# Sliding-window attention and an MLP on one core: another order of the first six blocks, and another queue for weights and casts

## The chip, the cores and the metric

The kernel runs on one core of one Trainium2 chip. The metric is the time of one execution in device microseconds, given as the median of several runs. TensorE (PE in the profile) does the matrix products and the transposes, VectorE (DVE), ScalarE (ACT) and GpSimd (POOL) do the element-wise work, and SyncE (SP) only issues transfers. GpSimd issues transfers too, on a queue of its own; only its transfers can convert fp32 to fp16 on the way.

## The reference

The inputs are q, k and v of shape (8, 8, 576, 64) in fp32: 8 sequences, 8 heads, 576 positions, 64 columns per head. The attention is causal with a window of 128 positions and a linear bias for each head. Its result, all heads side by side, gives x of shape (8, 576, 512), which goes through a normalised two-layer MLP with a residual.

```python
scores = scale * np.matmul(q, k.transpose(0, 1, 3, 2))
bias = slopes[:, None, None] * (-np.abs(rel).astype(np.float32))[None, :, :]
mask = (rel >= 0) & (rel < window)                  # window = 128
attn = softmax(np.where(mask, scores + bias[None], -1e9))
x = np.matmul(attn, v)                              # then heads side by side: (B, S, 512)
xn = (x - mu) / np.sqrt(var + 1e-06) * g_ln         # over the 512 columns
out = x + np.maximum(xn @ w_ch1, 0.0) @ w_ch2       # 512 -> 2048 -> 512
```

## The kernel before

**Blocks.** The 8 x 576 positions are cut into 36 blocks of 128 rows. Nine blocks (PERIOD) are a pair of sequences: with r the block's number within the pair, r from 0 to 3 are rows of the first sequence, r = 4 is half of either sequence, r from 5 to 8 are rows of the second one. Because of the window a block looks only at itself and at the block before it; with r = 0 there is none before it, and the block has half the work in scores, exponentials and P·V.

**Attention of a block** (function `attention`). q and k must stand with the head's columns on the partitions (tile qkt). This is reached in one of three ways. In a *span* (`SPANS`, lines 608 to 656) two neighbouring blocks are loaded together by SP into fp32 tiles qs and ks, so that one run in memory is 512 bytes (line 459); they are cast to fp16 (line 621, written `cT`), two fp16 values are taken as one fp32 word and transposed by PE (line 639, `T`), and copied out of PSUM (lines 648 and 650). A block outside the spans and below `LOAD_CAST` is loaded by SP (line 364), cast (line 560), and transposed by PE (line 687); from `LOAD_CAST` on, q and k are loaded as fp16 by GpSimd's queue (line 473), and from `QK_BY_DMA` on the transposition is a DMA transpose on SP's queue (line 702). v is loaded by SP and cast (lines 591 and 593) below `V_CAST`, and comes as fp16 by GpSimd's queue into tile vx from there on. The scores are written to the PSUM tiles sc0 and sc1 (line 725). For the first `BY_BIAS` = 5 blocks the bias is added by matrix products with a distance table (line 741); later blocks multiply the exponentials (line 773) by a mask (line 780). P·V (line 797) carries a column of ones, so that the sum of a row comes with it; its reciprocal (line 814) and the division (line 818) give xb, 16-bit. The mean is subtracted and the gain g multiplied (line 858, tile xs), and xs is transposed to xt, by PE for blocks below `X_BY_DMA` (lines 872 to 882) and by a DMA transpose on SP's queue from there on (line 887).

**The MLP** (function `mlp`) works on chunks of 2 to 4 blocks (`CHUNKS`). Phase A multiplies the chunk's xt by 16 slices of the first matrix (line 919, tasks `A`), with ReLU on ScalarE or VectorE (lines 929 and 931); phase B multiplies by the second matrix (line 947, tasks `B`), and line 955 scales by the standard deviation's inverse and adds the residual. The division by the standard deviation thus comes after both products. Each matrix comes in four quarters on GpSimd's queue, w0 to w3 for the first and w4 to w7 for the second. `W_AFTER` gives behind which load or cast each quarter is issued: position 3 i is q of block i, 3 i + 1 is k, 3 i + 2 is v.

**The order** of all instructions is made when the program is built. Every step is a task with an engine, a cost, what it depends on and a priority; class `Plan` runs through the tasks with these costs in an event loop, and the order in which it starts them is the order in each engine's queue. On the chip the engines wait for semaphores, but never change this order. `PICK` names the engines that may do a task, `PRI` shifts priorities, `HOLD` keeps a task back until a time of the plan, `SLACK` is a reserve after what PE waits for, and `rates` and `LANDING` stand for the speed of the transfer queues. Before `WARM`, PE's planned pauses are filled with products of a zero tile (line 986, L986 in the profile). Rings of tiles (class `Ring`) give block i the tile i modulo the ring's length; a write waits for the readers of the tile's last owner.

## Time and profile before

| | |
|---|---|
| time, median of 6 runs | 320.26 us (319.88 to 321.63) |
| the profiled execution: its time | 320.56 us |
| the profiled execution: its span | 318.8 us |
| PE busy | 308.6 us, 97% of the span |
| products of the MLP (L919, L947) | 135.7 + 135.7 us |
| P·V (L797), scores (L725, two groups) | 28.4, 19.7 + 18.4 us |
| products of the zero tile (L986) | 7.4 us, 76 of them |
| granted PE clock | 0.999 |

The page shows the span of one execution, which is a little shorter than its time. An engine's busy time is the union of its instructions; for PE it contains the products of the zero tile, which compute nothing. A wait is told with the engine and line that waited, and what ended the wait. "to landing" of a transfer runs from its issue to the moment its data are there. POOLq and SPq are the instructions with which GpSimd and SyncE issue transfers.

### The profile page before, as it was taken

The page shows a single profiled execution, that of the slowest core. Times are in us where ns is not written, and L with a number is a line of the kernel's source. Part 1 is how long each engine was busy: PE and PEld are TensorE (multiplying, and loading weights), DVE is VectorE, ACT ScalarE, POOL GpSimd, SP SyncE. Part 2 cuts the span into 40 slices and gives each one's busy share as a digit, 9 for nine tenths or more (in the row PEclk, how much of TensorE's full clock was granted, in tenths as well). Part 3 has the DMA queues.
Part 4 walks back from the last instruction along what each step waited for, and adds up shares of the span by engine and source line. Part 5 has one row for each costly group of instructions (what it writes and reads, how often), then busy time and mean ns, then how long its engine had stood idle before and what let it go on. Part 6 is the DMA issues. An engine that isn't in the chain of part 4 may idle for free.

```text
span 318.8 us, 6461 instructions
## 1 busy us (share of the span) xinstructions
PE 308.6 (97%) x2526; PEld 174.9 (55%) x2526; DVE 184.8 (58%) x511; ACT 164.6 (52%) x269; POOL 98.9 (31%) x131
## 2 busy tenths in 40 slices
PE   8969989999999999999999999999999999999995
PEld 6746866556655554554555545554555455445543
DVE  3669558874599648664866486548664866111012
ACT  2759875445656742474257525752575257305600
POOL 5735476673564256353433231001000000000000
PEclk9999999999999999999999999999999999999999
DMA  8999999999999999999999998627710221011011
GB/s 197 233 189 230 210 210 174 156 184 174 157 141 168 150 174 161 182 185 147 164 213 99 100 165 166 50 49 135 131 19 16 85 82 19 17 68 67 0 66 68
DMA packets 153906, 41.47 MB, mean 130 GB/s; under 512 B 138385, under 2 KB 148881, under 8 KB 153874
## 3 DMA queue, kind: packets, MB, share of 16 engines
q0 software_dynamic: 91232, 15.34, 68.8%
q1 hardware_dynamic: 62640, 25.70, 42.2%
q8 instruction: 20, 0.33, 0.5%
q14 instruction: 12, 0.10, 0.1%
q10 hardware_dynamic: 2, 0.00, 0.0%
HBM read 36.70 MB, written 9.44 MB: 145 GB/s over the span
## 4 chain that ended last, share of the span: by engine, by line
PE 86%; DMA 7%; SPq 5%; POOL 0%; issue 0%; DVE 0%; POOLq 0%
PE fb L947 39%; PE fb L919 36%; PE sc L725 5%; PE fb L797 5%; DMA w1sb<-in_moe_w_ch_dram 5%; SPq L364 3%; DMA qs<-in_q_dram 3%; SPq L459 2%; PE fb L872 1%; PE fb L639 0%; POOL vx L473 0%; POOL qs L621 0%; DVE ot L955 0%; POOLq L621 0%
## 5 line engine op out<-in xcount | busy, mean ns | idle before, releaser
L919 PE MATMUL fb<-xt,w1sb 128*128 128x512 f16 (+2 forms) x640 | 135.7, 359 | 1.0 <-DMA w1sb<-in_moe_w_ch_dram 1.0
L947 PE MATMUL fb<-w2sb,ht 128*128 128x512 f16 (+2 forms) x592 | 135.7, 373 | 0.0
L931 ACT ACTIVATE ht<-fb 128x512 f16<-128x512 f32 (+2 forms) x145 | 80.9, 560 | 62.9 <-PE fb L919 61.7
L773 ACT ACTIVATE probs<-sc 128x1024 f16<-128x1024 f32 (+1 forms) x72 | 67.6, 973 | 54.8 <-PE sc L725 54.7
L919 PEld LDWEIGHTS <-w1sb 128*128 128x128 f16 x640 | 68.3, 114 | 47.7 <-DMA w1sb<-in_moe_w_ch_dram 1.2
L947 PEld LDWEIGHTS <-ht 128*128 128x128 f16 x592 | 54.1, 98 | 56.9
L955 DVE SCALAR_TENSOR_TENSOR ot<-fb,rstd,xb 128x512 f32<-128x512 f32 (+2 forms) x37 | 27.2, 736 | 53.9 <-PE fb L947 53.3
L473 POOL DMA_DIRECT2D vx<-in_v_dram x34 | 28.8, 847 | 71.1 <-PE fb L797 64.0
L780 DVE TENSOR_TENSOR probs<-probs,mreg 128x1024 f16<-128x1024 f16 (+1 forms) x48 | 31.4, 656 | 28.7 <-ACT probs L773 28.4
L797 PEld LDWEIGHTS <-probs 128*128 128x128 f16 x544 | 25.4, 98 | 14.1 <-ACT probs L773 0.4
L818 DVE SCALAR_TENSOR_TENSOR xb<-fb,rec 128x256 f16<-128x256 f32 x72 | 30.5, 423 | 2.0
L473 POOL DMA_DIRECT2D qk<-in_q_dram x30 | 25.4, 846 | 18.5 <-DMA qkt<-qk 6.5
L473 POOL DMA_DIRECT2D qk<-in_k_dram x30 | 25.4, 846 | 12.5 <-DMA vx<-in_v_dram 5.7
L797 PE MATMUL fb<-vx,probs 128*128 128x65 f16 x544 | 28.4, 193 | 0.1
L858 DVE SCALAR_TENSOR_TENSOR xs<-xb,mean,g_t 128x512 f16<-128x512 f16 x36 | 27.4, 761 | 0.7
L839 DVE BATCH_NORM_STATS2 st<-xb 128x6 f32<-128x512 f16 x36 | 24.5, 683 | 0.0
L814 DVE RECIPROCAL rec<-fb 128x4 f32<-128x4 f32 x72 | 13.0, 180 | 19.4 <-PE fb L797 18.8
L725 PEld LDWEIGHTS <-qkt 64*128 64x128 f16 x544 | 15.3, 94 | 12.3 <-issue 10.5
L725 PE MATMUL sc<-qkt 64*128 64x128 f16 x288 | 19.7, 216 | 0.0
L725 PE MATMUL sc<-qkt,qkt 64*128 64x128 f16 x256 | 18.4, 219 | 0.0
L929 DVE TENSOR_SCALAR ht<-fb 128x384 f16<-128x384 f32 (+2 forms) x15 | 8.5, 565 | 5.1 <-PE fb L919 4.3
L621 POOL CAST qs<-qs 128x512 f16<-128x512 f32 (+1 forms) x7 | 6.3, 899 | 9.8 <-DMA qs<-in_q_dram 9.8
(62 smaller groups left out, 120.7 us busy)
## 6 DMA issues: line engine op xcount, KB each, us to landing
out_dram<-ot SPq DMA_DIRECT2D x35, 256.0 KB, 3.5
vx<-in_v_dram POOLq DMA_DIRECT2D x28, 128.0 KB, 9.7
qk<-in_q_dram POOLq DMA_DIRECT2D x24, 128.0 KB, 11.0
qk<-in_k_dram POOLq DMA_DIRECT2D x24, 128.0 KB, 11.0
w1sb<-in_moe_w_ch_dram POOLq DMA_DIRECT2D x4, 512.0 KB, 10.7
w2sb<-in_moe_w_ch_dram POOLq DMA_DIRECT2D x4, 512.0 KB, 12.5
ks<-in_k_dram SPq DMA_DIRECT2D x6, 256.0 KB, 4.6
qs<-in_q_dram SPq DMA_DIRECT2D x6, 256.0 KB, 4.9
```

Source lines behind the costliest of these rows:

```text
L473: nc.gpsimd.dma_start(out=dst(p0, n), in_=src[b, :, s0 : s0 + n, :].rearrange("h p d -> p h d"))
L725: nc.tensor.matmul(scs[half][:, g, c0 : c0 + P], kt[rows, 1, hp, :], qkt[i][rows, 0, hp, :], start=not bias, stop=True, skip_group_check=True,
L773: nc.scalar.activation(out=o, in_=n_, func=AF.Exp, scale=inv_sqrt_d)
L780: en.tensor_tensor(out=pv, in0=pv, in1=mask[:, 2 * half : 2 * half + 2, :, lo:], op=ALU.mult)
L797: nc.tensor.matmul(pp[:, hh * (D + 1) : hh * (D + 1) + D + 1], probs[i][:, bank, slot, side * P : side * P + P], vx[i - 1 + side][:, h, 0 ...
L818: nc.vector.scalar_tensor_tensor(out=xb[i][:, 256 * half : 256 * half + 256].rearrange("p (h d) -> p h d", d=D), in0=pp[:, :, 0:D], scalar ...
L839: nc.vector.bn_stats(out=st[i][:, :], in_=xb[i][:, :])
L858: nc.vector.scalar_tensor_tensor(out=xs[i][:, :], in0=xb[i][:, :], scalar=mean[i][:, 0:1], in1=g_t[:, :], op0=ALU.subtract, op1=ALU.mult,)
L919: nc.tensor.matmul(fb[b][:, 0:n_], w1f[f // CB][:, kb, f % CB, :], xt[c][:, kb, 0:n_], start=(kb == 0), stop=(kb == NKB - 1),)
L931: nc.scalar.activation(out=ht[c][:, f, 0:n_], in_=src, func=AF.Relu)
L947: nc.tensor.matmul(pm[:, 0 : c1 - c0], ht[c][:, f, j * P : j * P + P], w2sb[f // CB][:, f % CB, c0:c1], start=(f == 0), stop=(f == NFB - 1),)
L955: nc.vector.scalar_tensor_tensor(out=ot[i][:, c0:c1], in0=fb[plan.held[key][1]][:, 0 : c1 - c0], scalar=rstd[c][:, j : j + 1], in1=xb[i][: ...
```

## The change

The blocks are worked on in another order. `BLOCK[i]` is the block at place i: first blocks 0 and 1, 9 and 10, 18 and 19 (the first two of the first three pairs of sequences, `HEADS` = 3), then all others in their order. Whatever is indexed by place stays so (rings, chunks, spans); memory addresses, r and the block before go through `BLOCK` and `PLACE`. The tiles vx and qkt of places 1, 3 and 5, whose next block comes much later, are pinned, outside their rings.

The places 0 to 5 are three spans (`SPANS` from [0, 2, 5, 7] to [0, 2, 4]). From place 6 on q and k come as fp16 by GpSimd's queue (`LOAD_CAST` from 9 to 6), and v from place 1 on (`V_CAST` from 5 to 1). The weights' quarters are issued behind v2, v3 (four), v4 (two) and k6 (`W_AFTER`). q and k of places 6 to 11 are transposed by PE (`QK_BY_DMA` from 9 to 12), and xs by DMA from place 6 on (`X_BY_DMA` from 12 to 6). The first chunks are 3, 3 and 2 blocks instead of 3, 2 and 3. The tables `PICK` (engines per task), `PRI` and `HOLD` are others, and some costs of the plan: the shares of the queues, landing times of the first four places, the first transposition, the first quarter of weights, `SLACK` after 30 us from 0.2 to 1.0 and `WARM` from 22 to 24.

```diff
 class Ring:
+    def __init__(self, tiles, pins=None):
+        self.tiles, self.first, self.readers, self.pins = tiles, {}, {}, pins or {}
+    def turn(self, k):
+        return k - sum(1 for p in self.pins if p < k)
     def __getitem__(self, k):
-        return self.tiles[k % len(self.tiles)]
+        return self.pins[k] if k in self.pins else self.tiles[self.turn(k) % len(self.tiles)]
...
+    SHARES = {
+        (True, 512): (0.83, 0.28), (True, 256): (0.75, 0.2), (True, 2048): (0.7, 0.4),
+        (False, 512): (0.38, 0.62), (False, 256): (0.5, 0.5), (False, 2048): (0.5, 0.5),
+    }
...
-    CHUNKS = [3, 2, 3, 4, 4, 4, 4, 4, 4, 4]
+    CHUNKS = [3, 3, 2, 4, 4, 4, 4, 4, 4, 4]
...
-    WARM = 22.0
+    WARM = 24.0
...
-    MIX_AFTER = 4
+    MIX_AFTER = 3
     SPLIT = 4
-    LOAD_CAST = 9
-    V_CAST = 5
+    LOAD_CAST = 6
+    V_CAST = 1
...
-    SPANS = [0, 2, 5, 7]
-    SLACK = (0, 0.2, 0)
+    SPANS = [0, 2, 4]
+    SLACK = (0, 1.0, 0)
...
+    HEADS = 3
     BY_BIAS = 5
     MASK_AT = 5
-    QK_BY_DMA = 9
-    X_BY_DMA = 12
+    QK_BY_DMA = 12
+    X_BY_DMA = 6
...
+    BLOCK = [b for n in range(HEADS) for b in (PERIOD * n, PERIOD * n + 1)]
+    BLOCK += [b for b in range(NBLK) if b not in BLOCK]
+    PLACE = {b: i for i, b in enumerate(BLOCK)}
+    FAR = [i for i, b in enumerate(BLOCK) if b + 1 < NBLK and (b + 1) % PERIOD and PLACE[b + 1] > i + 1]
...
-    v32 = ring("v32", min(5, V_CAST), [P, H, D], FP32)
-    qk16 = ring("qk16", 6, [P, 2, d_model], FP16)
-    vx = ring("vx", 7 if V_CAST > 4 else 9, [P, H, VD], FP16)
-    qkt = ring("qkt", 6, [P, 2, HP, P], FP16)
+    v32 = ring("v32", min(4, V_CAST), [P, H, D], FP32)
+    qk16 = ring("qk16", 5, [P, 2, d_model], FP16)
+    vx = ring("vx", 7 if V_CAST > 4 else 9, [P, H, VD], FP16, FAR)
+    qkt = ring("qkt", 6, [P, 2, HP, P], FP16, FAR)
...
-        b0, r = 2 * (i // PERIOD), i % PERIOD
+        b0, r = 2 * (BLOCK[i] // PERIOD), BLOCK[i] % PERIOD
...
-    W_AFTER = [6, 12, 17, 18, 21, 22, 22, 28]
+    W_AFTER = [8, 9, 10, 10, 10, 12, 12, 19]
...
-            t_w[n] = plan.transfer(f"w{n}", "POOL", 0.8, 3.2 if n < 4 else 2.7, 0.0, emit, [casts[at % 3]] + last, av(i, -60.0))
+            t_w[n] = plan.transfer(f"w{n}", "POOL", 0.8, (3.2 if n else 4.2) if n < 4 else 2.7, 0.0, emit, [casts[at % 3]] + last, av(i, -60.0))
...
-        r = i % PERIOD
+        r = BLOCK[i] % PERIOD
+        before = PLACE[BLOCK[i] - 1] if r else None
...
-                                kt = qkt[i - 1 + side]
+                                kt = qkt[i if side else before]
...
-                            vx[i - 1 + side][:, h, 0 : D + 1],
+                            vx[i if side else before][:, h, 0 : D + 1],
...
-                    nc.sync.dma_start(out=out_flat[i * P : i * P + P, c0:c1], in_=ot[i][:, c0:c1])
+                    nc.sync.dma_start(out=out_flat[BLOCK[i] * P : BLOCK[i] * P + P, c0:c1], in_=ot[i][:, c0:c1])
```

## The prediction

> **What bounds the kernel now.** I read the page first: which engine has no slack, and when.
>
> ```profile
> span 318.8 us, 6461 instructions
> PE 308.6 (97%) x2526; PEld 174.9 (55%) x2526; DVE 184.8 (58%) x511; ACT 164.6 (52%) x269; POOL 98.9 (31%) x131
> ...
> PE   8969989999999999999999999999999999999995
> ...
> DMA  8999999999999999999999998627710221011011
> ...
> PE 86%; DMA 7%; SPq 5%; POOL 0%; issue 0%; DVE 0%; POOLq 0%
> ```
>
> PE is full from the sixth slice (8 us each) to the last. A change to the order can only win what PE loses in the first 42 us, where the chain leaves PE. The chain in order of time names the places, and the waits of PE (us in total, times, longest) and its timeline (start, duration) size them:
>
> ```profile
> 17.16 8.21 DMA qs<-in_q_dram
> ...
> 27.06 14.63 DMA w1sb<-in_moe_w_ch_dram
> 41.74 2.14 PE fb L919 x12
> ```
>
> ```profile
> PE fb L687 <- POOL qk L560: 2.7, 1, 2.7
> PE fb L639 <- POOL qs L621: 1.1, 2, 0.7
> PE fb L986 <- DVE warm_t L376: 1.1, 1, 1.1
> PE fb L919 <- DMA w1sb<-in_moe_w_ch_dram: 1.0, 1, 1.0
> PE fb L872 <- DVE xs L858: 0.7, 1, 0.7
> ```
>
> ```profile
> 4.30 0.76 PE L741 MATMUL sc<-dist_t,sid 128*128 128x128 f16 x8
> ...
> 22.92 0.40 PE L687 MATMUL fb<-iden,qk 128*128 128x128 f16 x4 [2.74 <-POOL qk L560]
> ...
> 25.25 0.84 PE L919 MATMUL fb<-xt,w1sb 128*128 128x384 f16 x4
> ...
> 41.74 2.14 PE L919 MATMUL fb<-xt,w1sb 128*128 128x384 f16 x12 [0.98 <-DMA w1sb<-in_moe_w_ch_dram]
> ```
>
> Read: first useful matmul at 4.30, first MLP matmul at 25.25, dense after 41.74. The filler (L986) hides losses that the page counts as busy. Between 4.3 and 41.74 I add the gaps and the stretches of filler: 4.6 us of filler and small waits up to 23.3, 2.9 around the late k cast of block 4 (22.92), 0.74 at 26.83, 0.98 at 41.74: **9.3 us lost**. The last matmul ends 3.4 us before the end. So the span is 4.3 + 301.8 (PE's real work) + 9.3 + 3.4 = 318.8.
>
> **The change, part by part.** The sum is made against the profiled execution (span 318.8, time 320.56, which lies 0.30 above the median of 320.26).
>
> *PE's work.* Bias matmuls (L741) are made for places 0 to 4 in both kernels. Before, these are one block without a predecessor and four with one: 0.60 (4.30 to the next instruction at 4.90) + 4 x 1.06 (four matmuls of 256 columns go from 9.54 to 10.07) = 4.8. After, three are without and two with: 3.9. So -0.9. Transposes of q and k on PE: four spans at 0.92 (12.42 to 12.88 is half of one) and one plain block at 0.46 before; three spans and six plain blocks (places 6 to 11, L687) after: 4.1 to 5.5, so +1.4. Transposes of xs (L872): twelve blocks to six, 0.28 each (0.23 to 0.33 in the timeline), -1.7. Scores and P·V keep their number, since four blocks in 36 have no predecessor in either order. Sum **-1.2**: 300.6. The six extra copies out of PSUM (L697, 1.02 on ScalarE) and six copies fewer of xt (0.4 to 0.6) lie beside PE, with ScalarE 22.3 us busy of the 40 between 60 and 100; without that cover they cost some 2 us.
>
> *DMA.* Landing times of before (issue plus time to landing): halves of a span (256 KB) come 0.9 to 1.1 us apart while SP's queue is alone (3.9, 4.75, 5.85, 7.0; 10.2, 11.0, 12.0, 12.9), v by SP 1.04 and 1.26, a casting load of 128 KB by POOL 0.85 (50.9, 51.7, 52.55), a quarter of W2 alone 2.3 and 2.6 (45.1, 47.4, 50.0). The four quarters of W1 land at 21.9, 28.2, 35.0 and 41.7; in the 19.8 us from the first to the last, three of them, two v and eight halves land, so a W1 quarter beside SP costs (19.8 - 8 x 0.95 - 2 x 0.85)/3 = 3.5.
>
> Of POOL's queue, the dependencies give the order v1, v2, w0, v3, w1 to w4, v4, w5, w6, v5, q6, k6, w7 (places, not blocks). Ahead of w3's landing stand twelve halves (11.4), v0 (1.1), v1 to v3 (2.6) and four quarters (14): 29.1 after a start at 2.9, so **w3 lands at 32**, 9.7 us earlier than now, w4 at 34.5, w5 38, w6 40, v5 41, w7 45 (now 55.0). The price stands in front: the halves of the second span now share the engines with v1, v2 and w0. The last of them lands at 12.9 now. After: 8 halves and v0 are 8.7, v1 and v2 1.7, so 13.3 if no weight gets ahead, and 17.7 if w0 and v3 do (+3.5 +0.85). POOL issues in order at 0.53 to 0.92 each: whatever cast of qs or ks stands behind such an issue is late by it, and the thirteen weights and v issued here pass POOL's casts of the second span. POOL also waits for old transfers: in the trace a q issue at 55.74 waits 1.65 for w7, the transfer eight issues earlier; in the new order the one eight before v4 is v1, landed long ago, so this costs nothing before 41.
>
> The Trainium skill (DMA: Bandwidth & Descriptors, Specifications) puts line rate at 512 B and more and a read-modify-write below, which speaks against casting loads whose rows are 128 B in SBUF. The 0.85 against 1.04 to 1.26 for uncast rows of 256 B shows no such cost here; were each of the five v twice a plain load (2.3), w7 would be 7 us later by that estimate.
>
> *When the MLP begins.* From the landing of the second span's last half to the third block's xt, the chain of before is 12.9 to 21.3 (xs of its third block ends at 20.46, transposition and copy 0.8): 8.4, with a full block and full ScalarE. After, the third block has no predecessor: cast 0.8, transposes 0.45, copy 0.6, scores 0.28, exp 0.6, P·V 0.13, reciprocal and division 0.7, mean 0.2, xs 0.75, transpose and copy 0.75, with waits about 6. So the MLP starts between 13.3 + 6 = 19.3 and 17.7 + 1.2 (a share of w1) + 8.4 = 27.3. Neither end is nearer to a row, so I take the middle, **23.4** (now 25.25).
>
> *Loss.* By then PE can have done G 1.1, two spans 1.8, bias 3.9, scores of four blocks 1.7, P·V of four 1.5, three xs transposes 0.8: 10.8. Lost: 23.4 - 4.3 - 10.8 = 8.3. The other limit is w3: before 32 PE has in addition three quarters of chunk 0 (16 matmuls go from 28.21 to 30.81, 2.6 each) and 2.0 of attention, 20.6 in all: 32 - 4.3 - 20.6 = 7.1, less than 8.3, so it doesn't bind. After that each W2 quarter (2.5) feeds 2.6 us of chunk 0, and v5 at 41 gives chunk 1 by about 45, when w7 lands. For a mismatch of a fixed order with such narrow margins I add 0.7 (before: 0.74 + 0.98 after its start); ends 0 and 2.5. X = **9.0** instead of 9.3.
>
> The Trainium skill (SBUF — State Buffer, SBUF: two separate sides) says that VectorE's two-port operations keep GpSimd from writing descriptors, so its DMAs wait. Rows: issues between 25 and 42, with VectorE busy 11.7 of 16.5 us, take 0.53 to 0.92, the later ones 0.85 to 0.93. By the rule, thirteen issues each behind half a cast of 0.46 would add an estimated 3 us.
>
> Sum: 4.3 + 300.6 + 9.0 + 3.4 = **317.3**, 1.5 less than 318.8; as a median **318.8**.
>
> **Rivals.**
> *The queue of weights makes the first chunk late (slower).* Place: SP's q and k of the second span against w0 and v3. For it: w0 to w3 land 6.3 to 6.8 apart now beside SP, so both slow down; against: POOL's casts stand between its issues, which holds weights back. At 27.3 and 0.7, X is 12.9, the time 322.7 (with 2.5: 324.5). It decides from a first MLP matmul after about 25.9 on.
> *xs behind q and k on SP's queue (slower).* From place 6 on xs goes by DMA transposes of SP, in one order with those of q and k from 12 on, which wait for POOL's loads. For it: SP's longest wait for such a load is 23.3 us, one issue takes 1.2 to 4.5, and xt transposes between 100 and 108 land after 8.5. Against: chunk 2 is needed only at about 70. Price 2 to 4.5: 320.8 to 323.3.
> *The holes only move (same).* The late k cast goes, but the wait for the second span takes its place: start at 24.9, 320.3.
>
> **How the numbers follow.** A measurement tells about 0.3% (1 us) from no change. Forecast (start before 23.9) 0.46; late first chunk 0.20; SP's queue 0.14; holes move 0.20. The forecast's own range: from a start at 19.3, where w3 binds (7.1, or 5.5 if it lands at 30.4), 313.8 + 1.5 = 315.3, to 319.2. With the slower ones up to 322.7 and part of the 2.5: 315.3 to 323.5.
>
> **What would show it.** Right: w3 landed near 32 and w7 near 45, first MLP matmul at 22 to 24, no wait of PE on L687 of 2 us, L741 at 24 matmuls of 128 columns and 16 of 256, L872 24 times, PE dense from about 35. Wrong: POOL or ScalarE casts of the second span after 19, a PE wait over 2 us for W2 or vx between 33 and 46, or for xt at 60 to 80.

## The result, and the profile after

The changed kernel takes 319.99 us (median of 28 runs, 319.11 to 321.69), the kernel before 320.59 us (56 runs beside them). The ratio is 0.9981 with a 95% interval of 0.9972 to 0.9990: a gain of 0.6 us, where 1.5 us had been forecast. The profiled execution has a time of 319.18 and a span of 317.5 us. That is almost the span that was forecast (317.3), but the execution stands 0.8 under its median. Read alone it would confirm the forecast; the median doesn't. Two of the twelve runs of after_third, below, took some 403 us at a granted clock of 0.76, and its ratio leaves them out.

The page of the changed kernel, in the same parts that were shown of before (span, busy times, slices of 8 us, shares of the chain that ended last):

```profile
span 317.5 us, 6575 instructions
PE 310.6 (98%) x2580; PEld 177.2 (56%) x2580; DVE 189.9 (60%) x523; ACT 161.0 (51%) x258; POOL 100.6 (32%) x133
...
PE   7899999999999999999999999999999999999995
...
PE 93%; DMA 3%; DVE 1%; SPq 1%; ACT 1%; issue 0%; DVEq 0%
```

PE's share of the chain went from 86 to 93%. The chain in order of time, over the first 14 us (start, duration), shows what is left of the transfers in it; then come the waits of PE (us in total, times, longest) and its timeline (start, duration, what; in brackets the idle time before it):

```profile
4.13 8.53 DMA ks<-in_k_dram
12.68 0.79 ACT ks L646
13.51 0.44 PE fb L666 x2
```

```profile
PE fb L666 <- POOL qs L648: 1.2, 1, 1.2
PE fb L1011 <- DVE warm_t L400: 1.1, 1, 1.1
PE sc L766 <- DVE sid L454: 0.5, 1, 0.5
PE fb L666 <- ACT ks L646: 0.3, 1, 0.3
```

```profile
3.23 1.58 PE L766 MATMUL sc<-dist_t,sid 128*128 128x128 f16 x8 [0.49 <-DVE sid L454]
...
8.47 0.44 PE L666 MATMUL fb<-iden,qs 128*128 128x128 f32 x2 [1.24 <-POOL qs L648]
...
18.37 0.44 PE L666 MATMUL fb<-iden,qs 128*128 128x128 f32 x2
...
20.33 0.19 PE L822 MATMUL fb<-vxp,probs 128*128 128x65 f16 x1
...
24.21 2.11 PE L944 MATMUL fb<-xt,w1sb 128*128 128x384 f16 x12
...
43.31 1.02 PE L972 MATMUL fb<-w2sb,ht 128*128 128x512 f16 x4 [0.17 <-DVE xb L843]
```

Compared with before:

- The wait of 2.74 for the late cast of k is gone, and no quarter of a weight is waited for. w3 has landed at about 29.6 (41.7 before) and w7 at 43.0 (55.0 before): 29.93 when it is issued, and 13.1 to landing.
- After its first MLP matmul (L944) PE waits 0.17 us in all, where before it waited 0.74 and 0.98.
- The first MLP matmul comes at 24.21 instead of 25.25, though the first transposes come at 8.47 instead of 5.62. The filler grew from 76 matmuls (7.4 us) to 122 (9.5 us): the loss lies earlier now, and nearly all of it ahead of the first MLP matmul.

So one quantity is enough to follow the result: span = start of the first MLP matmul + what remains. What remains was 318.8 - 25.25 = 293.55 before and is 317.5 - 24.21 = 293.3 after. The whole gain of this pair of executions, 1.3, is the earlier start (1.04) and 0.25 behind it.

The open question is why the median gains only 0.6, and what sets the start. POOL's timeline shows the two things that compete there:

```profile
7.66 0.75 POOL L648 CAST qs<-qs 128x512 f16<-128x512 f32 x1 [2.50 <-DMA qs<-in_q_dram]
8.33 0.76 POOL L562 DMA_DIRECT2D w1sb<-in_moe_w_ch_dram  x1
9.08 0.89 POOL L499 DMA_DIRECT2D vxp<-in_v_dram  x1
13.51 0.76 POOL L648 CAST qs<-qs 128x512 f16<-128x512 f32 x1 [3.54 <-DMA qs<-in_q_dram]
14.19 0.76 POOL L562 DMA_DIRECT2D w1sb<-in_moe_w_ch_dram  x1
15.69 0.77 POOL L648 CAST ks<-ks 128x512 f16<-128x512 f32 x1 [0.74 <-DMA ks<-in_k_dram]
```

w0 and v of place 3 (called v3 below, tile vxp) are issued at 8.33 and 9.08, behind a cast that itself waits for the first span, and their transfers run beside SP's second span, whose last half is cast at 15.69. v3 lands 11.2 us after its issue, at 20.29; the first product of P·V of place 3 that reads it starts at 20.33. There is nothing to spare.

### The profile page after: what moved, and what is told of

The parts are those of the page before. It is cut to its first block, busy times and chain, and to the rows that moved or that the text cites. A ratio compares the mean times of both kernels' runs of the same rounds, so it can differ in the third digit from the quotient of the medians.

```text
span 317.5 us, 6575 instructions
## 1 busy us (share of the span) xinstructions
PE 310.6 (98%) x2580; PEld 177.2 (56%) x2580; DVE 189.9 (60%) x523; ACT 161.0 (51%) x258; POOL 100.6 (32%) x133
## 4 chain that ended last, share of the span: by engine, by line
PE 93%; DMA 3%; DVE 1%; SPq 1%; ACT 1%; issue 0%; DVEq 0%
PE fb L944 40%; PE fb L972 39%; PE sc L750 6%; PE fb L822 5%; DMA ks<-in_k_dram 3%; PE fb L714 1%; SPq L483 1%; PE fb L1011 1%; PE sc L766 1%; PE fb L666 1%; PE fb L897 0%; ACT probs L798 0%; ACT ks L646 0%; DVE mmix L469 0%; DVE st L864 0%
## 5 line engine op out<-in xcount | busy, mean ns | idle before, releaser
L944 PE MATMUL fb<-xt,w1sb 128*128 128x512 f16 (+2 forms) x640 | 134.6, 359 | 0.0
L956 ACT ACTIVATE ht<-fb 128x512 f16<-128x512 f32 (+2 forms) x142 | 79.5, 560 | 52.4 <-PE fb L944 50.7
L944 PEld LDWEIGHTS <-w1sb 128*128 128x128 f16 x640 | 68.9, 114 | 47.1
L980 DVE SCALAR_TENSOR_TENSOR ot<-fb,rstd,xb 128x512 f32<-128x512 f32 (+2 forms) x37 | 27.2, 736 | 42.1 <-PE fb L972 41.7
L499 POOL DMA_DIRECT2D qk<-in_q_dram x34 | 28.7, 845 | 45.4 <-DMA qkt<-qk 34.2
L499 POOL DMA_DIRECT2D vx<-in_v_dram x36 | 30.4, 849 | 35.5 <-PE fb L822 18.9
L805 DVE TENSOR_TENSOR probs<-probs,mreg 128x1024 f16<-128x1024 f16 (+1 forms) x46 | 30.3, 676 | 13.9 <-ACT probs L798 13.8
L839 DVE RECIPROCAL rec<-fb 128x4 f32<-128x4 f32 x72 | 12.7, 179 | 36.3 <-PE fb L822 35.9
L822 PEld LDWEIGHTS <-probs 128*128 128x128 f16 x544 | 24.9, 97 | 12.7 <-ACT probs L798 0.2
L499 POOL DMA_DIRECT2D qk<-in_k_dram x34 | 28.6, 843 | 6.3 <-DMA w1sb<-in_moe_w_ch_dram 2.0
L822 PE MATMUL fb<-vx,probs 128*128 128x65 f16 x496 | 27.2, 193 | 0.1
L750 PE MATMUL sc<-qkt 64*128 64x128 f16 x264 | 18.0, 216 | 0.0
L750 PE MATMUL sc<-qkt,qkt 64*128 64x128 f16 x208 | 14.7, 219 | 0.0
L954 DVE TENSOR_SCALAR ht<-fb 128x384 f16<-128x384 f32 (+2 forms) x18 | 10.4, 579 | 6.3 <-PE fb L944 6.0
L1011 PE MATMUL fb<-warm_t 128*128 128x128 f16 x122 | 9.5, 234 | 1.1 <-DVE warm_t L400 1.1
## 6 DMA issues: line engine op xcount, KB each, us to landing
w2sb<-in_moe_w_ch_dram POOLq DMA_DIRECT2D x4, 512.0 KB, 13.3
```

The source lines that it names most:

```text
L499: nc.gpsimd.dma_start(out=dst(p0, n), in_=src[b, :, s0 : s0 + n, :].rearrange("h p d -> p h d"))
L750: nc.tensor.matmul(scs[half][:, g, c0 : c0 + P], kt[rows, 1, hp, :], qkt[i][rows, 0, hp, :], start=not bias, stop=True, skip_group_check=True,
L805: en.tensor_tensor(out=pv, in0=pv, in1=mask[:, 2 * half : 2 * half + 2, :, lo:], op=ALU.mult)
L822: nc.tensor.matmul(pp[:, hh * (D + 1) : hh * (D + 1) + D + 1], probs[i][:, bank, slot, side * P : side * P + P], vx[i if side else before] ...
L944: nc.tensor.matmul(fb[b][:, 0:n_], w1f[f // CB][:, kb, f % CB, :], xt[c][:, kb, 0:n_], start=(kb == 0), stop=(kb == NKB - 1),)
L956: nc.scalar.activation(out=ht[c][:, f, 0:n_], in_=src, func=AF.Relu)
```

## The experiments

All ratios are to the kernel before on the same chip, as they stand on record; they are not the quotients of two medians (for after_again 319.86 and 320.15 would give 0.9991). "Start" is that of the first MLP matmul in the one profiled execution, and "remains" is that execution's span less the start. "Theory" and "rival" are the two outcomes that each expectation sets against each other.

| run | time us | ratio (95%) | start | remains |
|---|---|---|---|---|
| changed kernel | 319.99 | 0.9981 (0.9972 to 0.9990) | 24.21 | 293.3 |
| after_again | 319.86 | 0.9998 (0.9979 to 1.0017) | 24.43 | 293.4 |
| after_third | 319.89 | 0.9978 (0.9952 to 1.0004) | 24.65 | 293.45 |
| before_again | 320.24 | 1.0002 (0.9986 to 1.0019) | 24.90 | 293.5 |
| v0_behind | 320.93 | 1.0025 (1.0012 to 1.0038) | 25.35 | 294.05 |
| w0_held | 323.59 | 1.0095 (1.0069 to 1.0121) | 25.28 | 297.8 |
| v3_first | 319.36 | 0.9973 (0.9953 to 0.9993) | 23.77 | 294.1 |
| w_late | 331.59 | 1.0341 (1.0302 to 1.0380) | 27.17 | 303.6 |
| v_by_sp | 322.11 | 1.0056 (1.0036 to 1.0077) | 27.47 | 292.6 |
| x12 | 321.11 | 1.0024 (1.0008 to 1.0040) | 24.01 | 295.3 |
| qk9 | 318.97 | 0.9967 (0.9954 to 0.9981) | 24.88 | 292.4 |
| v3_first_qk9 | 319.06 | 0.9968 (0.9949 to 0.9986) | 23.35 | 293.35 |
| heads2 | 320.80 | 1.0016 (0.9999 to 1.0033) | 26.79 | 293.4 |

### The same two kernels, profiled again

Edit: none. The changed kernel ran twice more (after_again, after_third), the kernel before once more (before_again).

> The changed kernel once more, unaltered. The question is why its profiled execution has a span 1.3 us shorter than before, but its median time only 0.6 us. Theory A (jitter before the MLP): the first landings vary from one execution to the next, so the first MLP matmul of this execution comes at another moment than 24.2, by up to 1 us, and its span differs from 317.5 by the same amount, with PE's waits after it still below 0.5 us. Theory B (narrow margins after it): the first MLP matmul stays at 24.2 within 0.3 and PE waits 0.5 to 1.5 us for a quarter of the weights or a v between 28 and 46. Theory C: the profiled execution is an ordinary one, spans stay at 317.5 within 0.3, and the medians will differ by 1.3 when both are taken on one chip.

> The changed kernel a third time, unaltered. In three profiled executions with its order of the first 24 us, PE waited 0, 0.62 and 1.22 us at about 20 for v of place 3, which GpSimd issues behind the first quarter of weights, and the first MLP matmul came at 24.21, 24.43 and 24.88. Theory A (this landing varies, and the execution shown first was a lucky one): a wait of 0.3 to 1.3 again, first MLP matmul at 24.3 to 25.0, span 317.6 to 318.3. Rival: no wait and a span of 317.5 within 0.2; then the smaller gain of the medians has another cause.

> The kernel of before once more, unaltered, as the measure of how far two medians of one kernel lie apart: theories A, B and C all expect a ratio of 1.000 within 0.001. For its profiled execution, A expects the first MLP matmul off 25.25 by up to 1 us; B and C expect it at 25.25 within 0.3, with the waits of 2.7 for the late k and of 1.0 for the fourth quarter again.

Measured: spans of 317.8 and 318.1 for the changed kernel, 318.4 for the one before. PE's timeline of after_again, and then of after_third:

```profile
20.56 0.19 PE L822 MATMUL fb<-vxp,probs 128*128 128x65 f16 x1 [0.62 <-DMA vxp<-in_v_dram]
...
24.43 2.11 PE L944 MATMUL fb<-xt,w1sb 128*128 128x384 f16 x12
```

```profile
20.77 0.19 PE L822 MATMUL fb<-vxp,probs 128*128 128x65 f16 x1 [0.68 <-DMA vxp<-in_v_dram]
...
24.65 2.11 PE L944 MATMUL fb<-xt,w1sb 128*128 128x384 f16 x12
```

The issue of v3 on POOL, in after_again and in after_third:

```profile
9.30 0.89 POOL L499 DMA_DIRECT2D vxp<-in_v_dram  x1
```

```profile
9.54 0.89 POOL L499 DMA_DIRECT2D vxp<-in_v_dram  x1
```

What follows: the profiled execution was a good one. P·V of place 3 waits 0 in it, 0.62 and 0.68 in the other two, and the start moves along: 24.21, 24.43, 24.65. Theory A holds. What varies is the issue of v3, 9.08, 9.30 and 9.54: POOL stands in order behind its cast of the first span's q, whose data land at 7.61, 7.83 and 8.07. From the issue v3 takes 11.2 us each time. It lands at 20.29, 20.52 and 20.73 (issue plus time to landing), and the start follows that by 3.92, 3.91 and 3.92. The two other executions with this order up to the start, x12 and qk9 below, have v3 at 20.09 and 20.96 and the start 3.92 later as well. So in the changed kernel the start hangs on v3. The second span doesn't hold it up there: in the later two its last half is there earlier (its cast on POOL follows without a wait, at 14.57 and 14.59, where the good execution has it at 15.69 after a wait of 0.74). What remains is the same within 0.15. Over the three executions the span is 317.8, over the two of before 318.6: -0.8, near the medians' -0.6. On the chip of after_again alone no gain can be told (0.9998, 0.9979 to 1.0017).

PE's timeline of before_again has the waits of before in their places, 2.43 for the late k and 1.12 after the start. The row of the second one names VectorE, but the last quarter of W1 lands at 41.33 there, 0.05 before the wait ends. The waits belong to the kernel:

```profile
22.57 0.40 PE L687 MATMUL fb<-iden,qk 128*128 128x128 f16 x4 [2.43 <-POOL qk L560]
...
41.38 2.14 PE L919 MATMUL fb<-xt,w1sb 128*128 128x384 f16 x12 [1.12 <-DVE probs L780]
```

### v0_behind: the first span ahead of v of place 0

```diff
-    PRI = {..., 'qs0.0.i': 1.7, ..., 'v0.i': -6.1, ...}
+    PRI = {..., 'qs0.0.i': -3.4, ..., 'v0.i': 3.0, ...}
```

SP issues the first span's halves first, and v of place 0 behind them.

> The changed kernel with SP's first load, v of place 0, issued behind the four halves of the first span, and q's first half ahead of its second. Theory 1 (the start binds: after the first MLP matmul PE is dense, so each us by which that comes earlier is a us won): first transposes at 5.6 instead of 8.5, first MLP matmul at 23 instead of 24.2, time 1 us less than the changed kernel, ratio to before 0.995. Theory 2 (the weights bind just as much: w3 at 29.6 and w7 at 43.0 don't move): the earlier start is given back in waits for weights, ratio 0.998 as for the changed kernel.

Measured: 1.0025. The first transposes come at 5.93 instead of 8.47, but the first MLP matmul at 25.35 instead of 24.21. Neither theory's numbers were met. POOL's timeline:

```profile
6.21 0.76 POOL L562 DMA_DIRECT2D w1sb<-in_moe_w_ch_dram  x1
6.95 0.90 POOL L499 DMA_DIRECT2D vxp<-in_v_dram  x1
16.99 0.76 POOL L648 CAST qs<-qs 128x512 f16<-128x512 f32 x1 [9.14 <-DMA qs<-in_q_dram]
18.42 0.77 POOL L648 CAST ks<-ks 128x512 f16<-128x512 f32 x1
```

What follows: POOL's first cast hardly waits for its data any more (0.17 instead of 2.50), so w0 and v3 behind it are issued 2.1 us earlier (6.21, 6.95 against 8.33, 9.08). They then run against the second span, whose casts on POOL slip from 13.51 and 15.69 to 16.99 and 18.42, with a wait of 9.14. The wait of 2.50 in the changed kernel is a brake for the weights. This is the prediction's slower rival, the queue of weights that makes the first chunk late, seen at work. Here v3 isn't what the start hangs on: it lands at 19.22, and its product starts without a wait.

### w0_held: the same, with the first quarter held back

```diff
-    PRI = {..., 'qs0.0.i': 1.7, ..., 'v0.i': -6.1, ...}
+    PRI = {..., 'qs0.0.i': -3.4, ..., 'v0.i': 3.0, ...}
-    HOLD = {'Za0': 3.13, 'k10.i': 55.05, 'cT0.11': 9.73, 'mreg20': 36.97, 'k8.i': 46.36, 'dist2a': 4.68}
+    HOLD = {'Za0': 3.13, 'w0.i': 13.0, 'k10.i': 55.05, 'cT0.11': 9.73, 'mreg20': 36.97, 'k8.i': 46.36, 'dist2a': 4.68}
```

> The order of loads of the run with v of place 0 behind the first span, and in addition GpSimd issues the first quarter of weights only behind two casts of the second span (about 13 instead of 6 to 8). In the run before it, POOL stopped waiting for the first span's cast, issued w0 and v3 two us earlier, and the second span's casts fell from 13.5 and 15.7 to 17.0 and 18.4, the first MLP matmul from 24.2 to 25.3. Theory 1 (weights and second span share one capacity, and both limits are close together): the second span's last cast is done by 15, the first MLP matmul comes at 22 to 23.5, but w0 to w7 land 2 to 4 us later, so PE then waits 2 to 5 us for weights or for v4 and v5, and the time is 1 to 5 us longer than the changed kernel: ratio to before 1.002 to 1.014. Theory 2 (only the first chunk's start binds): the earlier start is kept, ratio 0.993 to 0.996. Theory 3 (the weights do not slow the second span; another cause made the start later in the run before): first MLP matmul stays at 25 or later.

Measured: 1.0095. POOL's timeline, and PE's later on:

```profile
13.15 0.75 POOL L648 CAST qs<-qs 128x512 f16<-128x512 f32 x1 [0.96 <-DMA qs<-in_q_dram]
13.83 0.76 POOL L562 DMA_DIRECT2D w1sb<-in_moe_w_ch_dram  x1
14.58 0.77 POOL L648 CAST ks<-ks 128x512 f16<-128x512 f32 x1
17.30 0.89 POOL L499 DMA_DIRECT2D vxp<-in_v_dram  x1
```

```profile
47.94 0.19 PE L822 MATMUL fb<-vx,probs 128*128 128x65 f16 x1 [1.03 <-DVE xb L843]
...
49.08 0.61 PE L714 MATMUL fb<-iden,qk 128*128 128x128 f16 x8 [0.74 <-DVE xb L843]
...
50.72 0.38 PE L897 MATMUL fb<-iden,xs 128*128 128x128 f16 x4 [1.03 <-DVE qkt L722]
```

What follows: the second span's casts are back at 13.15 and 14.58 and its transposes come at 16.31 (18.37 in the changed kernel), so w0 and v3 did delay it in v0_behind, and the cause that theory 3 assumed is out, though its number (a start of 25 or later) came true. The time lies in theory 1's range, but the start, 25.28, is no better (its 22 to 23.5 was missed), and PE waits for no weight. v3 is issued only at 17.30 and w0 lands at 21.0; that the plan lays PE's order out for these late loads, and so makes the start late, is argued. A second cause isn't told apart: the granted PE clock of this execution is 0.67, 0.50 and 0.98 in the three stretches of 2 us from 10 to 16. After the start four waits follow, 0.81, 1.03, 0.74 and 1.03. The first transfers or the weights came early here, not both. The median is of 4 runs, and the profiled execution (324.87) is the slowest of them.

### v3_first: v of place 3 ahead of the first quarter

```diff
-    W_AFTER = [8, 9, 10, 10, 10, 12, 12, 19]
+    W_AFTER = [11, 11, 11, 11, 11, 12, 12, 19]
```

All of w0 to w4 are issued behind v3.

> The changed kernel with one place of GpSimd's queue exchanged: v of place 3 ahead of the first quarter of weights instead of behind it. Theory A (the wait for that v is what the typical execution loses against the one profiled first, and weights ahead of the second span's halves delay the chunk): no wait for vx at 20, the second span's last transposes at 15 to 17 instead of 18.4, first MLP matmul at 22.8 to 23.8, w0 landed by 21, and the time 0.5 to 1.5 us less than the changed kernel: ratio to before 0.993 to 0.997. Rival (the weights are late by what the start is early): PE waits 0.5 to 1.5 us for them between 25 and 46, ratio 0.997 to 1.000.

Measured: 0.9973, on a chip where the changed kernel has 0.9978. PE's timeline:

```profile
23.77 1.46 PE L944 MATMUL fb<-xt,w1sb 128*128 128x384 f16 x8
...
28.32 0.44 PE L666 MATMUL fb<-iden,ks 128*128 128x128 f32 x2 [0.70 <-POOL ks L648]
...
44.18 1.02 PE L972 MATMUL fb<-w2sb,ht 128*128 128x512 f16 x4 [0.57 <-DVE xb L843]
```

What follows: the wait for v3 is gone, the second span's transposes come at 15.47, and the start at 23.77, 0.66 ahead of the mean of the changed kernel's three (24.43). Then 0.70 and 0.57 are given back at 28.32 and 44.18: 294.1 remain instead of 293.4. Theory A's start came true (22.8 to 23.8), the rival's price came true too, though what PE waits for are casts and VectorE, not weights. The edit moves two things, v3 and the second span's transposes, so it doesn't price v3 alone. The times of the two kernels can't be told apart.

### w_late: the weights' quarters behind the places they had before

```diff
-    W_AFTER = [8, 9, 10, 10, 10, 12, 12, 19]
+    W_AFTER = [8, 12, 17, 18, 21, 22, 22, 28]
```

> The changed kernel with the weights' quarters behind the same positions as before the change, except the first (behind v2, k of place 4, v5, q6, q7 twice, and k9). Theory 1 (the earlier weights carry the gain of the new order): w3 lands at 36 or later instead of 29.6, w7 at 55 or later instead of 43, and PE waits 5 to 13 us for them: ratio to before 1.015 to 1.04. Rival (the weights are hidden anyway: PE has blocks 3 to 6 to do meanwhile): PE waits under 2 us, ratio 0.998 to 1.004.

Measured: 1.0341 (4 runs). PE's timeline ahead of the start, and the longest waits of PE between 24 and 80 us:

```profile
22.02 0.19 PE L822 MATMUL fb<-vxp,probs 128*128 128x65 f16 x1 [2.19 <-DMA vxp<-in_v_dram]
```

```profile
PE fb L944 <- DVE qkt L722: 2.4, 2, 1.6
PE fb L822 <- ACT qkt L724: 2.1, 1, 2.1
PE fb L822 <- DVE probs L805: 1.5, 2, 1.0
```

What follows: the start goes to 27.17, with a wait of 2.19 for v3 ahead of it, and 303.6 remain instead of 293.4. The time lies in theory 1's range, but not by the waits that it names: w3 lands at 32.97 and w7 at 53.84 (36 and 55 or later were expected), and none of PE's waits ends with a weight. With the quarters late, the plan puts attention ahead of the MLP in PE's order, and PE waits for steps of VectorE and ScalarE in it; that reading is argued from the waits. Part of what remains is the clock's, with 0.50 granted at 68 to 70. So with this order of blocks early quarters are a condition, not an extra. What early quarters would bring in the old order wasn't run, and so the gain can't be divided between the two.

### v_by_sp: v of places 1 to 5 by SP again

```diff
-    V_CAST = 1
+    V_CAST = 6
```

These v come in fp32 on SP's queue and are cast by an engine, as before.

> The changed kernel with v of places 0 to 5 loaded by SP as fp32 and cast, as before the change, instead of places 1 to 5 by GpSimd's queue as fp16. Theory 1 (a casting load costs the transfer engines less than a plain one, 0.85 against 1.04 to 1.26, and v in front of the weights delays both alike): the five loads cost 1 to 2 us more of transfer time and five casts of 0.6 on GpSimd or ScalarE; w7 lands 1 to 3 us later; 0.5 to 2 us longer than the changed kernel: ratio to before 1.000 to 1.005. Rival (the queue doesn't matter, only the bytes read): the same time as the changed kernel, ratio 0.998.

Measured: 1.0056, slightly above the range of theory 1 (1.000 to 1.005). PE's timeline:

```profile
27.47 0.81 PE L944 MATMUL fb<-xt,w1sb 128*128 128x384 f16 x4 [0.36 <-ACT xt L907]
```

What follows: the start moves by 3.0 from the mean of 24.43; what remains doesn't get longer (292.6). The choice is thus worth some 2.4 us (1.0056 against 0.9981), all of it ahead of the start, and the rival's number, no difference, is out. w7 lands at 45.20 instead of 43.05, within theory 1's 1 to 3 us. Why it is worth that isn't shown: the edit moves the casts as well as the transfers, w0 is issued at 14.00 instead of 8.33 since it stands behind v2, and the granted PE clock of this execution is 0.50 at 10 to 12 and 0.64 at 12 to 14.

### x12 and qk9: work of PE given back, or taken away

```diff
-    X_BY_DMA = 6
+    X_BY_DMA = 12
```

> The changed kernel with xs of places 6 to 11 transposed by PE again, as before the change, instead of by DMA. Theory 1 (PE is dense, its work counts one to one): six blocks at 0.28, 1.7 us longer than the changed kernel, ratio to before 1.003 to 1.004. Rival (transposes by DMA come late on SP's queue and cost PE as much in waits as they save): no difference, ratio 0.998.

```diff
-    QK_BY_DMA = 12
+    QK_BY_DMA = 9
```

> The changed kernel with q and k of places 9 to 11 transposed by DMA again, as before the change, instead of by PE. Theory 1 (PE's work counts one to one): three blocks at 0.46 us leave PE, so 1.4 us less than the changed kernel, ratio to before 0.994. Rival (SP's queue: transposes of q and k stand ahead of those of xs and wait for GpSimd's loads): a PE wait for xt of 1 to 4 us between 60 and 90, ratio 0.998 to 1.008.

Measured: x12 1.0024, qk9 0.9967. In x12 PE transposes xs of six more blocks. The start is 24.01, and 295.3 remain instead of 293.3: +2.0, where the step of the prediction had 1.7 for these blocks. Its ratio is just below theory 1's 1.003 to 1.004, with an interval that holds it. In qk9 three blocks' q and k are transposed by DMA instead of PE; 292.4 remain instead of 293.4, where 1.4 was to go; 0.9967 lies between theory 1's 0.994 and the rival's 0.998, and neither came true. PE's timeline of qk9, and its waits between 26 and 110 us:

```profile
21.01 0.19 PE L822 MATMUL fb<-vxp,probs 128*128 128x65 f16 x1 [1.22 <-DMA vxp<-in_v_dram]
```

```profile
PE sc L750 <- DMA qkt<-qk: 0.4, 1, 0.4
```

What follows: behind the start PE's work counts about one to one. Of the 1.4 that qk9 takes from PE, 0.4 comes back as a wait for the DMA transpose. Its profiled execution had the longest wait for v3 (1.22) of the five with the same order up to the start. On one chip qk9 takes 318.97 beside 319.86 for the changed kernel, and its interval (up to 0.9981) hardly touches that of after_again there (from 0.9979). Its ratio is the lowest of the single edits, but v3_first's interval (0.9953 to 0.9993) holds it.

### v3_first_qk9: both edits

```diff
-    QK_BY_DMA = 12
+    QK_BY_DMA = 9
-    W_AFTER = [8, 9, 10, 10, 10, 12, 12, 19]
+    W_AFTER = [11, 11, 11, 11, 11, 12, 12, 19]
```

> Both edits that theory holds to be gains: v of place 3 ahead of the first quarter of weights, and q and k of places 9 to 11 transposed by DMA. If they add, 1.0 (measured for the transposes: 317.3 - 24.88 = 292.4 after the first MLP matmul instead of 293.3) and 0.5 to 1.5 less than the changed kernel: ratio to before 0.990 to 0.994. If the earlier start only meets the same limit of the weights: 0.996 to 0.997, as for the transposes alone.

Measured: 0.9968, with the earliest start of all, 23.35, in an execution (318.41) that stands 0.65 under its median.

What follows: the two gains don't add. 293.35 remain, 0.75 less than in v3_first, but 0.95 more than in qk9: waits of 0.9 for the DMA transposes and 0.57 at 42.85 take the earlier start back. It is the second case of the expectation (0.996 to 0.997). In time, there is nothing to choose between it and qk9 alone.

### heads2: two pairs ahead instead of three

```diff
-    HEADS = 3
+    HEADS = 2
```

> The changed kernel with the first two blocks of two pairs of sequences ahead instead of three, so that place 4 is a block with a predecessor. Theory 1 (a block without a predecessor among the first five saves PE its half of the bias products and of scores, exponentials and P.V while the first weights come): bias 0.46 us more on PE, scores and P.V of place 4 0.5 more before 40 (and as much less later), so 0.4 to 1.0 us longer than the changed kernel, ratio to before 0.999 to 1.002. Rival (the order of blocks doesn't matter for PE, since all work is done in the end): 0.998, as for the changed kernel, within 0.001.

Measured: 1.0016 (0.9999 to 1.0033). PE's timeline:

```profile
22.22 0.19 PE L822 MATMUL fb<-vxp,probs 128*128 128x65 f16 x1 [2.21 <-DMA vxp<-in_v_dram]
```

What follows: 293.4 remain, as in the changed kernel, and the start is 26.79, 2.4 later, with a wait of 2.21 for the same v3. The ratio is within the range of theory 1, but the row shows another cause than its half block of work: v3 lands 12.7 us after its issue instead of 11.2, and why is open. The profiled execution (321.86) also stands 1.06 above its median, so 2.4 is more than the edit costs. In this execution the start moves and nothing behind it. It ran with the tables of priorities made for three pairs, so it doesn't show what two pairs could reach at best.

## Why the prediction was right or wrong

**The time: wrong in size.** Forecast 318.8 as a median, 1.5 less than before; measured 0.6 less. 319.99 is inside the range, the direction is right, and the gain, 0.2%, is less than the 0.3% from which the prediction itself tells a change. (The middle of its 19.3 and 27.3 is 23.3, not 23.4; that changes nothing here.)

**The failing step: "Neither end is nearer to a row, so I take the middle, 23.4".** The start was 24.21, 24.43 and 24.65, a mean of 24.43: 1.0 too early in the forecast. By its own bound, the case "start before 23.9" did not come true, and the rival "the holes only move", with a start of 24.9, was nearer. Two rows say what the middle left out.

- v3. The step counted "P·V of four" as work done by the start, and asked when the second span lands, but not when v of place 3 does. The prediction's own order of POOL's queue puts v3 behind w0, and P·V of place 3 stands in PE's order ahead of the first MLP matmul. By its own prices all loads up to v3 have landed at 17.7 (13.3 + 3.5 + 0.85); v3 landed at 20.29, 20.52 and 20.73, and the start came 3.92, 3.91 and 3.92 after that. The sum of 17.7 leaves out that SP issues its third span from 8.44 on and POOL the next quarter at 14.19, ahead of v3's landing; how much of the lateness is theirs isn't shown. P·V waits 0, 0.62 and 0.68, 0.43 in the mean, and up to 2.21 in heads2.
- PE's fixed order. The landing itself was well placed: the last half's cast begins at 15.69 (and at 14.57 and 14.59), where the middle of 13.3 and 17.7 is 15.5. But its transposes run at 18.37, 1.9 us after that cast ends (17.93 and 18.08 in the others), because scores, bias and P·V of the places before stand ahead of them. This limit comes second to that of v3: without the waits for v3 the three starts would be 24.21, 23.81 and 23.97 at best, 24.0 in the mean (an estimate, from the starts less the waits). In v3_first, where the transposes run at 15.47 and v3 is there, the start is 23.77, near the forecast.

So the wait for v3 is 0.43 of the 1.0. That PE's order makes up the other 0.6 is argued, not shown: no run moved the transposes alone.

**The loss after the start: also off, the other way.** "For a mismatch of a fixed order with such narrow margins I add 0.7": it was 0.17 in the first profile, 0.3 in the two others, none of them for weights or v. What remains is 293.3 to 293.45 against the forecast's 317.3 - 23.4 = 293.9. So +1.0 at the start and -0.5 behind it give a span of 317.8 in the mean, where 317.3 was forecast.

**The base: 0.2 too high.** The sum was made against the profiled execution of before, with a span of 318.8. The second one has 318.4, so the mean is 318.6. Together with the 0.5 of the last paragraph that is the difference between 1.5 and 0.8; the medians give 0.6.

**PE's work, -1.2: right as far as it was tested.** L766 has 24 matmuls of 128 columns and 16 of 256, and L897 24, all as forecast. The prices held: six blocks of xs by PE cost 2.0 in x12 (forecast 1.7), three blocks of q and k gave 0.9 to 1.0 plus a wait of 0.4 in qk9 (forecast 1.4).

**The weights: right, and earlier than forecast.** w3 at 29.6 (forecast 32), w7 at 43.0 (45). PE is dense from 24.21 on, where "from about 35" had been written. w_late shows that the new order needs them early. One reading was wrong without harm: that POOL's waits for old transfers cost "nothing before 41". POOL's issues of k of place 6 and of w7 wait 1.99 and 1.63 us, at 27.42 and 29.93, but no wait of PE comes of it.

**The rivals.** *The queue of weights makes the first chunk late*: not in the changed kernel, but in v0_behind, with a start of 25.35. That is short of the 25.9 from which it was to decide, and it costs 1.0025 all the same, because a wait after the start comes on top (1.03 at 48.39; 294.05 remain). *xs behind q and k on SP's queue*: no run of the changed kernel shows a wait of PE for xt, and x12, which takes those of places 6 to 11 away, is slower. *The holes only move*: the nearest in time (320.3), and the nearest at the start; but the wait that took the late k's place is the one for v3, not the one for the second span that it named.

**Short rows, and VectorE beside GpSimd.** The Trainium skill (DMA: Bandwidth & Descriptors, Specifications) puts line rate at transfers of 512 B and more and a read-modify-write below, which spoke against casting loads with rows of 128 B in SBUF. v_by_sp took those casting loads away and was slower, 1.0056. Its plain loads have rows of 256 B, below 512 too, so the rule itself wasn't tested; as a guide for this choice it pointed the wrong way. The Trainium skill (SBUF — State Buffer, SBUF: two separate sides) says that VectorE's two-port operations keep GpSimd from writing descriptors. The early issues of weights and v on POOL took 0.54 to 1.05 us with VectorE at work, and w7 landed before its forecast; no run here shows that cost.

## What to carry to other kernels

When a stage starts on the last of several loads, list every load that stands ahead of it in the engine's order and give each its landing time; a middle between two ends for the biggest one misses the small one behind it on the other queue. Two queues that load at once can slow each other (in v0_behind w0 and v3 were issued 2.1 us earlier, and the second span's casts slipped from 13.51 and 15.69 to 16.99 and 18.42): before an edit moves the first load forward, ask what it lets through behind it (here a cast that waited was what held the weights back). And profile an execution a second time when a gain of 0.5% is in question: one of the three spans here agreed with the forecast, their mean did not.

## What the runs showed of the hardware

**A landing that varies, and what it carries along.** The half of the first span's q that SP issues at 2.48 landed at 7.61, 7.83 and 8.07 in three executions of the same kernel. The cast, the issue of v3 behind it, the landing of v3 and the first MLP matmul each came later by the same amounts, 0.22 to 0.23 us in the second execution and 0.44 to 0.46 in the third. Why the first landing varies is open.

**An issue that waits for the transfer eight before it.** In the changed kernel the issue of k of place 6 at 27.42 waits 1.99 for w1sb, and that of w7 at 29.93 waits 1.63. On POOL's queue the transfers eight issues earlier are w2, which lands at 27.13, and w3, at 29.65. Whether the chip or the way in which the program is built sets the eight isn't shown:

```profile
27.42 0.88 POOL L499 DMA_DIRECT2D qk<-in_k_dram  x1 [1.99 <-DMA w1sb<-in_moe_w_ch_dram]
29.93 0.56 POOL L564 DMA_DIRECT2D w2sb<-in_moe_w_ch_dram  x1 [1.63 <-DMA w1sb<-in_moe_w_ch_dram]
```

**A clock that fell behind short waits, and one that didn't.** In w0_held the three waits between 46.9 and 50.7 (2.8 us) are followed by a granted PE clock of 0.50, as the table of stretches shows (stretch, its length, PE's busy time and matmuls, granted clock; the last two columns, on transfers, aren't used here):

```profile
48.00:50.00 2.00, 0.95 (x16) 1.00 2.23 142
50.00:52.00 2.00, 1.28 (x22) 0.91 1.45 93
52.00:54.00 2.00, 2.00 (x7) 0.50 1.86 125
54.00:56.00 2.00, 2.00 (x10) 0.74 2.24 143
```

Four matmuls of 512 columns take 1.88 us at 51.59 and 1.03 at 56.31. So the 297.8 that remain there, 4.4 more than in the changed kernel, are more than the 3.6 us of its four waits. But waits alone don't tell when: in w_late three waits between 41.5 and 46.5 (1.58, 0.58 and 1.00) left the clock at 1.00 up to 66, and in w0_held it was 0.50 at 12 to 14 already, though after the first 1.06 us no wait ahead of that is longer than 0.49. No rule comes out of these rows.
